# An attention and gating network on one core: weight conversion in four steps, and SyncE's queue in program order

## The chip, the cores and the metric

The kernel runs on one core of a Trainium2 chip. The metric is the device time of one execution in microseconds (us). TensorE (PE) does the matrix products, VectorE (DVE) and ScalarE (ACT) the work on single elements, GpSimd (POOL) a few small things, and SyncE (SP) issues most DMA transfers. Each engine works through its own instructions in order and waits for the others by semaphores.

## What is computed

Three stages follow each other, on 4 batches, 448 tokens, 12 heads of 64:

```python
scores = q @ k.T / sqrt(64) - log(448)
x = sigmoid(scores) @ v                       # heads joined: 4 x 448 x 768
h = relu(x @ w_in); u, v = h[:512], h[512:]   # on the last axis
x = (u * (w_spatial @ layernorm(v) + b)) @ w_out
theta = x @ w_theta
y = x + w_tok_r @ (x * cos(theta)) + w_tok_i @ (x * sin(theta))
out = y + relu(y @ w_ch)
```

The weights come as 64-bit floats, q, k, v as 32-bit floats.

## The kernel before

**Products.** A 32-bit operand is split into a hi part, rounded to the format that TensorE multiplies fast, and a lo part, the rest; a product is three matmuls (hi hi, hi lo, lo hi). The hi part of a weight is a copy on ScalarE, the lo part a subtraction on VectorE.

**The attention stage** has 12 rounds, `r` = 0 to 11 (L363 to L403), three for each batch; a round takes two tiles of two heads each. In a round TensorE does, for the round after it (`nxt`), the scores of the last 64 rows (`end_scores`, tile `pse`), then for its own two tiles the product with v (`begin_attend`, `attend`, tile `psa`), then the scores of `nxt` (`scores`, tile `pss`, three for each tile). ScalarE makes a sigmoid of each score tile (L187) and copies each result to `X` (L60); VectorE makes the lo part of `X` and a small copy `XL` (L233). There are three score tiles in PSUM, so that the fourth matmul group of a round waits for a sigmoid. `split_pair` (L178) makes hi and lo of the keys and queries `kqr` of the round after next (`aft`), on VectorE. When the three rounds of a batch are through, its u and v products (`uv`, tile `psd`, with the parts `wih` and `wil` of `w_in`) are put on the list `todo`, and `uv_now` runs as many as `UV_BY` names for the round, once enough pieces are `finished`.

**The weight conversion** runs beside this. 39 pieces (12 of `w_in`, 27 of later weights) are loaded as 64-bit numbers (`load`, L96, tile `wraw`, four buffers) and turned into 32-bit ones by bit operations: `low` (two instructions on VectorE, L105 and L107, tile `wq`), `high` (ScalarE, L112, in place in `wraw`, so behind `low`), `join` (VectorE, L117, behind `high`). A piece of `w_in` then gets its hi part (`part_high`, L286, ScalarE) and its lo part (`part_low`, L290, VectorE, behind the hi part); any other piece is written to memory as 32-bit numbers (L282, called a spill here). `begin_pieces` and `end_pieces` are a step: in one step the pieces loaded before get `low` and `high`, and the pieces that had these before get join, hi part and lo part. A round has two steps, from round 3 on three.

**Order.** Inside the block at L347 the instructions of TensorE, ScalarE and VectorE stand in the order of the code. SyncE's DMAs are ordered by a planner, and can go out ahead of what stands before them in the code. Behind the block the planner orders all engines.

Of the kernel before, what the change touches and what calls it, by code (L numbers as in the profile page):

```python
# [18 lines left out]
B, H, S, D = 4, 12, 448, 64  # L19
NP = H // 2  # L20
# [18 lines left out]
CH_FROM = (1, 0)  # L39
NX = 12  # L40
NKQ = 3
UV_BY = (0, 0, 0, 3, 5, 7, 10, 13, 15, 18, 20)
NW = 4
NQ = 4
# [4 lines left out]
def net(ctx: ExitStack, tc: tile.TileContext, kq, vd, vl, w_in, w_sp, bsp, w_out, w_th, w_tok, w_ch, ident, out):  # L49
# [3 lines left out]
    def sub(o, a, b):  # L53
        ve.tensor_tensor(out=o, in0=a, in1=b, op=ALU.subtract)  # L54
# [23 lines left out]
    for i in range(2):  # L78
        t = const.tile([P, DH], F32R, name=f"vb{i}")
# [62 lines left out]
    def chunks(w):  # L142
        return w.rearrange("(c p) f -> p c f", p=P)
# [22 lines left out]
    def load_kq(n):  # L166
        b, p = divmod(n, NP)
        t = {"n": n, "a": {}, "fs": n in F32_SCORES}
        r = t["r"] = at.tile([P, 2, S], F32, tag="kqr", name="kqr", bufs=4)
        nc.sync.dma_start(r, kq[b, p])  # L170
        return t
# [6 lines left out]
    def split_pair(t):  # L178
        r = t["r"]
        hi = t["h"] = at.tile([P, 2, S], F32R, tag="kqh", name="kqh", bufs=NKQ)  # L180
        lo = t["l"] = at.tile([P, 2, S], F32R, tag="kql", name="kql", bufs=NKQ)
        ve.tensor_copy(hi, r)
        sub(lo, r, hi)

    def sigmoid(tag, ps, bufs):
        af = at.tile([P, 2, S], F32, tag=tag, name="af", bufs=bufs)
        se.activation(af, ps[:, :, :S], AF.Sigmoid, bias=bias, scale=1.0 / math.sqrt(D))  # L187
        return af

    def scores(t, g):  # L190

        ps = ps_s.tile([P, 2, 512], F32, tag="s", name="pss")
        c = slice(g * P, (g + 1) * P)
        if t["fs"]:
            for j, a in enumerate(halves):
                te.matmul(ps[:, j, :S], t["r"][a, 0, c], t["r"][a, 1, :], start=True, stop=True)
        else:
            for n, (w, x) in enumerate(("hh", "hl", "lh")):
                for j, a in enumerate(halves):
                    te.matmul(ps[:, j, :S], t[w][a, 0, c], t[x][a, 1, :], start=n == 0, stop=n == 2)  # L200
        t["a"][g] = sigmoid("af", ps, NAF)

    def end_scores(ts):

        ps = ps_s.tile([P, 2, 512], F32, tag="s", name="pse")
        for i, t in enumerate(ts):
            for j, a in enumerate(halves):
                te.matmul(ps[halves[i], j, :S], t["r"][a, 0, L0:S], t["r"][a, 1, :], start=True, stop=True)
        return sigmoid("afe", ps, 2)
# [3 lines left out]
    def begin_attend(ts, ends, ae):  # L213

        ps = [ps_m.tile([P, 512], F32, tag="m", name="psa") for _ in ts]
        for i, t in enumerate(ts):
            for j, a in enumerate(halves):
                te.matmul(ps[i][a, :S], ends[halves[i], t["n"] % NP // 2 * 2 + j, :], ae[halves[i], j, :],
                          start=True, stop=False)
        return ps  # L220
# [15 lines left out]
    def uv(b, g):  # L236
        ps = ps_m.tile([P, 512], F32, tag="m", name="psd")
        if g < 4:
            for k in range(KC):
                if g < 3:  # L240
                    xh, xlo = (xs[b, k][:, i, g * P:(g + 1) * P] for i in range(2))
                else:
                    xh, xlo = (xl[b // 2, k][:, i].rearrange("p b t -> p (b t)") for i in range(2))
                te.matmul(ps, xh, wih[:, k, DH:], start=k == 0, stop=False)
                te.matmul(ps, xh, wil[:, k, DH:], start=False, stop=False)
                te.matmul(ps, xlo, wih[:, k, DH:], start=False, stop=k == KC - 1)
            r = x_p.tile([P, DH], F32, tag="ev", name="ev", bufs=2)
            acopy(r, ps, AF.Relu)
            if g < 3:
                nc.scalar.dma_start(v_d[b][g * P:(g + 1) * P, :], r)  # L250
            else:
                nc.scalar.dma_start(v_d[b - 1][L0:S, :], r[0:64])
                nc.scalar.dma_start(v_d[b][L0:S, :], r[64:P])
        else:
            f = g - 4
            fs = slice(f * P, (f + 1) * P)
            for k in range(KC):
                X = xs[b, k]
                mm3(ps[:, :S], wih[:, k, fs], wil[:, k, fs], X[:, 0, :], X[:, 1, :], k == 0, k == KC - 1)
            r = x_p.tile([P, DH], F32, tag="ev", name="ev", bufs=2)  # L260
            acopy(r[:, :S], ps[:, :S], AF.Relu)
            nc.scalar.dma_start(u_d[b][fs, :], r[:, :S])
# [29 lines left out]
    pieces = [Piece(chunks(w_in), k, slice(o, o + DH)) for o in (DH, 0) for k in range(KC)]  # L292
# [12 lines left out]

    loaded, apart, joined = [], [], []
    todo = []
    N = B * NP
    finished = 0

    def load_pieces(n):
        for _ in range(n):
            if pieces:
                loaded.append(pieces.pop(0))
                loaded[-1].load()

    def begin_pieces(n):
        joined[:] = apart
        apart[:] = loaded
        loaded.clear()  # L320
        for w in joined:
            w.join()
        for w in apart:
            w.low()
        load_pieces(n)

    def end_pieces():
        nonlocal finished
        for w in apart:
            w.high()  # L330
        for w in joined:
            w.part_high()
        for w in joined:
            w.part_low()
        finished += len(joined)
        joined.clear()

    def uv_now(n):
        nonlocal groups
        for _ in range(n):  # L340
            if todo and finished >= (KC if todo[0][1] < 4 else 2 * KC):
                uv(*todo.pop(0))
                groups += 1

    R = B * NP // 2
    groups = 0
    with tc.manual_schedule(engines={mybir.EngineType.PE, mybir.EngineType.Activation, mybir.EngineType.DVE}):  # L347
        rounds = {r: [load_kq(2 * r + i) for i in range(2)] for r in range(1)}
        load_pieces(1)
        ends = load_ends(0)  # L350
        rounds[1] = [load_kq(2 + i) for i in range(2)]
        for t in rounds[0]:
            load_v(t)
        split_pair(rounds[0][1])
        for g in range(3):
            scores(rounds[0][0], g)
        ae = end_scores(rounds[0])
        for t in rounds[1]:
            split_pair(t)
        for g in range(3):  # L360
            scores(rounds[0][1], g)
        nc.sync.dma_start(idt, ident)
        for r in range(R):  # L363
            b, q = divmod(r, NP // 2)
            cur, nxt, aft = rounds.pop(r), rounds.get(r + 1), None
            last = r == R - 1
            if nxt:
                ends_n = load_ends(b + 1) if q == NP // 2 - 1 else ends
                ae_n = end_scores(nxt)
            begin_pieces(1)  # L370
            ps = begin_attend(cur, ends, ae)
            for t, o in zip(cur, ps):
                attend(t, o)
            if nxt:
                for t in nxt:
                    load_v(t)
                ends, ae = ends_n, ae_n
            if r + 2 < R:
                aft = rounds[r + 2] = [load_kq(2 * (r + 2) + i) for i in range(2)]
            if nxt:  # L380
                for g in range(3):
                    scores(nxt[0], g)
                for g in range(3):
                    scores(nxt[1], g)
            end_pieces()
            if q == NP // 2 - 1:
                todo += [(b, g) for g in range(8) if g != 3 or b % 2]
            if last:
                break
            if r >= NP // 2:  # L390
                begin_pieces(2 if r == NP // 2 else 1)
                if aft:
                    split_pair(aft[0])
                uv_now(1)
                end_pieces()
            elif aft:
                split_pair(aft[0])
            begin_pieces(1 if r < NP // 2 - 1 else 2)
            if aft:
                split_pair(aft[1])  # L400
            uv_now(UV_BY[r] - groups - 1)
            end_pieces()
            uv_now(UV_BY[r] - groups)  # L403
        while pieces or loaded or apart:
            begin_pieces(2)
            end_pieces()
    es_l.close()
# [259 lines left out]
    for b in range(B):  # L667
# [4 lines left out]
        for k in range(KC):  # L672
            nc.scalar.dma_start(yf[:, k, :], src[:, k, :])
            t = pc.tile([P, 2, S], F32R, tag="Y", name="Y", bufs=6)
# [3 lines left out]
        for e in range(KC):  # L678
# [4 lines left out]
            r = po.tile([P, S], F32, tag="o", name="o")  # L683
# [49 lines left out]
```

## Time and profile before

| | us |
|---|---|
| median of 3 runs | 656.89 |
| lowest and highest of them | 656.76, 657.71 |
| the profiled execution | 658.28 |
| its span, first to last instruction | 656.5 |

The profile comes from one execution. Its times are us from the start of the span; idle time stands in square brackets with what ended it. PEclk is the granted clock of TensorE as a share of full speed. Round r begins where the matmuls of L208 for round r+1 begin.

### The profile page before, as it was taken

What the parts mean: (1) busy time and instruction counts of PE and PEld (TensorE: products, weight loads), DVE (VectorE), ACT (ScalarE), POOL (GpSimd) and SP (SyncE); (2) the same over time, 40 slices, a digit from 0 to 9 for tenths busy, and PEclk for the clock granted to TensorE, in tenths of its full rate; (3) what the DMA queues carried; (4) which work ended last, traced back from release to release, by engine and by line L of the source; (5) the groups of instructions that cost most, each with busy time, mean ns of one, the idle gap of its engine ahead of it and who ended that gap; (6) DMA issues with size and microseconds to landing.
All of it is one profiled execution on the core that took longest, in us unless ns stands there. A gap on an engine that the chain in (4) does not pass through costs nothing.

```text
span 656.5 us, 9127 instructions
## 1 busy us (share of the span) xinstructions
PE 641.8 (98%) x3434; PEld 524.3 (80%) x3434; DVE 384.1 (59%) x747; ACT 286.0 (44%) x468; POOL 8.0 (1%) x18
## 2 busy tenths in 40 slices
PE   7999979999999999999999999999999999999997
PEld 3545656567656688899999999999999999899996
DVE  3657763545355368783315699998678765523311
ACT  5776546535553544274312554664344333302200
POOL 2000000000000000100000000000000000000000
PEclk9989979999999999999999999999999999999999
DMA  8754744685545466566454223351121012623411
GB/s 319 240 195 148 262 133 150 223 263 173 160 167 203 161 212 192 173 184 191 154 171 160 91 62 101 90 183 42 43 85 42 1 43 75 207 86 125 141 65 62
DMA packets 52368, 94.78 MB, mean 144 GB/s; under 512 B 8290, under 2 KB 38884, under 8 KB 52324
## 3 DMA queue, kind: packets, MB, share of 16 engines
q1 hardware_dynamic: 41060, 75.84, 35.8%
q10 hardware_dynamic: 11264, 18.36, 8.5%
q8 instruction: 27, 0.44, 0.3%
q14 instruction: 17, 0.14, 0.1%
HBM read 64.79 MB, written 29.39 MB: 143 GB/s over the span
## 4 chain that ended last, share of the span: by engine, by line
PE 87%; DVE 4%; ACT 3%; DMA 3%; issue 2%; POOL 0%; ACTq 0%; DVEq 0%; POOLq 0%
PE psa L225 7%; PE pss L200 5%; PE py L617 5%; PE py L618 5%; PE py L616 5%; PE pch L64 5%; PE pch L65 5%; PE pt L575 4%; PE pt L576 4%; PE pt L577 4%; PE pch L63 4%; PE ppo L65 3%; PE ppo L63 3%; PE ppo L64 3%; PE psd L63 2%; PE psd L65 2%
## 5 line engine op out<-in xcount | busy, mean ns | idle before, releaser
L187 ACT ACTIVATE af<-pss,bias 128x896 f32<-128x896 f32 x72 | 66.1, 1018 | 2.4 <-PE pss L200 2.4
L575 PE MATMUL pt<-thh,XT 128*128 128x384 f32 x168 | 58.2, 346 | 0.0
L225 PE MATMUL psa<-af,vr 128*64 128x448 f32 x288 | 56.8, 543 | 0.0
L577 PE MATMUL pt<-thh,XT 128*128 128x384 f32 x168 | 56.3, 335 | 0.0
L576 PE MATMUL pt<-thl,XT 128*128 128x384 f32 x168 | 56.3, 335 | 0.0
L64 PE MATMUL pch<-Y,wch 128*128 128x448 f32 x144 | 52.8, 369 | 0.4 <-DVE Y L54 0.4
L65 PE MATMUL pch<-Y,wcl 128*128 128x448 f32 x144 | 52.7, 368 | 0.0
L63 PE MATMUL pch<-Y,wch 128*128 128x448 f32 x144 | 52.2, 368 | 0.0
L117 DVE SCALAR_TENSOR_TENSOR wq<-wraw,wq 128x384 int32<-128x384 int32 (+2 forms) x51 | 29.6, 594 | 35.0 <-ACT wraw L112 34.6
L225 PEld LDWEIGHTS psa<-af,vr 128*64 128x64 f32 x288 | 19.6, 137 | 36.3 <-issue 34.5
L684 DVE SCALAR_TENSOR_TENSOR o<-pch,yf 128x448 f32<-128x448 f32 x24 | 15.0, 624 | 54.6 <-PE pch L65 54.6
L586 ACT ACTIVATE m<-r 128x384 f32<-128x384 f32 x28 | 14.6, 522 | 62.7 <-DVE r L584 62.3
L63 PE MATMUL psd<-X,wih 128*128 128x448 f32 x96 | 37.0, 385 | 3.3 <-ACT wih L60 3.2
L112 ACT ACTIVATE wraw<-wraw 128x384 f32<-128x384 f32 (+2 forms) x51 | 29.6, 604 | 22.3 <-DVE wq L105 16.8
L54 DVE TENSOR_TENSOR X<-psa,X 128x448 fp32r<-128x448 f32 x24 | 14.9, 623 | 38.6 <-ACT X L60 38.6
L65 PE MATMUL psd<-X,wil 128*128 128x448 f32 x96 | 36.2, 377 | 0.7 <-DVE wil L54 0.6
L60 ACT ACTIVATE ev<-psd 128x448 f32<-128x448 f32 (+1 forms) x30 | 17.0, 568 | 45.3 <-PE psd L65 19.9
L64 PE MATMUL psd<-X,wih 128*128 128x448 f32 x96 | 35.9, 374 | 0.0
L60 ACT ACTIVATE Y<-yf 128x448 fp32r<-128x448 f32 x24 | 13.9, 579 | 49.3 <-DMA yf<-y_d 28.9
L63 PE MATMUL ppo<-g,wbh 128*128 128x448 f32 x96 | 35.2, 366 | 0.0
L64 PE MATMUL ppo<-g,wbh 128*128 128x448 f32 x96 | 35.1, 366 | 0.0
L65 PE MATMUL ppo<-g,wbl 128*128 128x448 f32 x96 | 35.1, 366 | 0.0
(138 smaller groups left out, 1514.7 us busy)
## 6 DMA issues: line engine op xcount, KB each, us to landing
kqr<-in_kq SPq DMA_DIRECT2D x24, 448.0 KB, 5.0
wraw<-in_w_in SPq DMA_DIRECT2D x12, 512.0 KB, 5.4
x_d<-x ACTq DMA_DIRECT2D x24, 224.0 KB, 2.4
xf<-x_d SPq DMA_DIRECT2D x4, 1344.0 KB, 6.3
y_d<-y SPq DMA_DIRECT2D x24, 224.0 KB, 1.9
yf<-y_d ACTq DMA_DIRECT2D x24, 224.0 KB, 3.5
out_t<-o SPq DMA_DIRECT2D x24, 224.0 KB, 2.0
vr<-in_vd SPq DMA_DIRECT2D x24, 192.0 KB, 4.1
```

The source lines that it names most:

```text
L63: te.matmul(ps, wh, xh, start=first, stop=False)
L64: te.matmul(ps, wh, xl, start=False, stop=False)
L65: te.matmul(ps, wl, xh, start=False, stop=last)
L187: se.activation(af, ps[:, :, :S], AF.Sigmoid, bias=bias, scale=1.0 / math.sqrt(D))
L200: te.matmul(ps[:, j, :S], t[w][a, 0, c], t[x][a, 1, :], start=n == 0, stop=n == 2)
L225: te.matmul(ps[a, :S], t["v"][:, 2 * c + j, :], t["a"][c][:, j, :], start=False, stop=c == 2)
L575: te.matmul(o, t[:, k, 0, :], thh[:, k, hs], start=k == 0, stop=False)
L576: te.matmul(o, t[:, k, 0, :], thl[:, k, hs], start=False, stop=False)
L577: te.matmul(o, t[:, k, 1, :], thh[:, k, hs], start=False, stop=k == KC - 1)
L616: te.matmul(o, z[:, 0, ds], tkh[:, c, :], start=i == 0 and n == 0, stop=False)
L617: te.matmul(o, z[:, 0, ds], tkl[:, c, :], start=False, stop=False)
L618: te.matmul(o, z[:, 1, ds], tkh[:, c, :], start=False, stop=i == 3)
```

## The change

- The steps of a piece become four: load; `low` and `high`; join and hi part; lo part. `begin_pieces` first makes the lo parts of the pieces whose hi part was made in the step before, and counts them as finished; `end_pieces` makes hi parts, then `high`.
- In each round `end_pieces` of the first step stands directly behind `begin_pieces`, ahead of the attend matmuls and the X copies (before: behind the scores).
- Two pieces are loaded ahead of round 0 instead of one, both ahead of the v ends and of the second pair of keys and queries. `LOADS` gives the pieces of the second and third step of a round.
- Keys and queries of round r+3 are loaded in round r (before, in the code: of round r+2); v of round r+2 is loaded in round r (before: of r+1). The buffers stay four each.
- SyncE's DMAs inside the block stand in the order of the code, too.

```diff
@@ -39,6 +39,7 @@
 CH_FROM = (1, 0)
 NX = 12
 NKQ = 3
+LOADS = ((1, 0), (2, 0), (2, 0), (2, 2)) + 7 * ((1, 2),)
 UV_BY = (0, 0, 0, 3, 5, 7, 10, 13, 15, 18, 20)
 NW = 4
 NQ = 4
@@ -305,7 +306,6 @@
 
     loaded, apart, joined = [], [], []
     todo = []
-    N = B * NP
     finished = 0
 
     def load_pieces(n):
@@ -315,6 +315,11 @@
                 loaded[-1].load()
 
     def begin_pieces(n):
+
+        nonlocal finished
+        for w in joined:
+            w.part_low()
+        finished += len(joined)
         joined[:] = apart
         apart[:] = loaded
         loaded.clear()
@@ -325,15 +330,11 @@
         load_pieces(n)
 
     def end_pieces():
-        nonlocal finished
+
+        for w in joined:
+            w.part_high()
         for w in apart:
             w.high()
-        for w in joined:
-            w.part_high()
-        for w in joined:
-            w.part_low()
-        finished += len(joined)
-        joined.clear()
 
     def uv_now(n):
         nonlocal groups
@@ -344,17 +345,18 @@
 
     R = B * NP // 2
     groups = 0
-    with tc.manual_schedule(engines={mybir.EngineType.PE, mybir.EngineType.Activation, mybir.EngineType.DVE}):
-        rounds = {r: [load_kq(2 * r + i) for i in range(2)] for r in range(1)}
-        load_pieces(1)
+    with tc.manual_schedule(engines={mybir.EngineType.PE, mybir.EngineType.Activation, mybir.EngineType.DVE, mybir.EngineType.SP}):
+        rounds = {0: [load_kq(i) for i in range(2)]}
+        load_pieces(2)
         ends = load_ends(0)
         rounds[1] = [load_kq(2 + i) for i in range(2)]
-        for t in rounds[0]:
+        for t in rounds[0] + rounds[1]:
             load_v(t)
         split_pair(rounds[0][1])
         for g in range(3):
             scores(rounds[0][0], g)
         ae = end_scores(rounds[0])
+        rounds[2] = [load_kq(4 + i) for i in range(2)]
         for t in rounds[1]:
             split_pair(t)
         for g in range(3):
@@ -362,46 +364,42 @@
         nc.sync.dma_start(idt, ident)
         for r in range(R):
             b, q = divmod(r, NP // 2)
-            cur, nxt, aft = rounds.pop(r), rounds.get(r + 1), None
-            last = r == R - 1
+            cur, nxt, aft = (rounds.get(r + i) for i in range(3))
             if nxt:
                 ends_n = load_ends(b + 1) if q == NP // 2 - 1 else ends
                 ae_n = end_scores(nxt)
+            if r + 3 < R:
+                rounds[r + 3] = [load_kq(2 * (r + 3) + i) for i in range(2)]
             begin_pieces(1)
+            end_pieces()
             ps = begin_attend(cur, ends, ae)
             for t, o in zip(cur, ps):
                 attend(t, o)
-            if nxt:
-                for t in nxt:
+            if aft:
+                for t in aft:
                     load_v(t)
-                ends, ae = ends_n, ae_n
-            if r + 2 < R:
-                aft = rounds[r + 2] = [load_kq(2 * (r + 2) + i) for i in range(2)]
-            if nxt:
-                for g in range(3):
-                    scores(nxt[0], g)
-                for g in range(3):
-                    scores(nxt[1], g)
-            end_pieces()
             if q == NP // 2 - 1:
                 todo += [(b, g) for g in range(8) if g != 3 or b % 2]
-            if last:
+            if not nxt:
                 break
-            if r >= NP // 2:
-                begin_pieces(2 if r == NP // 2 else 1)
-                if aft:
-                    split_pair(aft[0])
-                uv_now(1)
-                end_pieces()
-            elif aft:
+            ends, ae = ends_n, ae_n
+            for t in nxt:
+                for g in range(3):
+                    scores(t, g)
+            begin_pieces(LOADS[r][0])
+            if aft:
                 split_pair(aft[0])
-            begin_pieces(1 if r < NP // 2 - 1 else 2)
+            end_pieces()
+            uv_now(min(1, UV_BY[r] - groups))
+            if LOADS[r][1]:
+                begin_pieces(LOADS[r][1])
             if aft:
                 split_pair(aft[1])
-            uv_now(UV_BY[r] - groups - 1)
-            end_pieces()
+            uv_now(min(1, UV_BY[r] - groups))
+            if LOADS[r][1]:
+                end_pieces()
             uv_now(UV_BY[r] - groups)
-        while pieces or loaded or apart:
+        while pieces or loaded or apart or joined:
             begin_pieces(2)
             end_pieces()
     es_l.close()
```

## Rows read from the trace of the kernel before

**Rows 1.** The page: busy us (share of the span) and instructions of each engine.

```profile
PE 641.8 (98%) x3434; PEld 524.3 (80%) x3434; DVE 384.1 (59%) x747; ACT 286.0 (44%) x468; POOL 8.0 (1%) x18
```

**Rows 2.** TensorE's waits (us, times, longest), up to 98.28 us; last row: from there on.

```profile
PE psd L63 <- ACT wih L60: 3.2, 2, 2.0
PE pss L200 <- ACT af L187: 1.9, 3, 0.9
...
PE pch L64 <- DVE Y L54: 0.4, 1, 0.4
```

**Rows 3.** Windows r1 to r5 (r3 in two): us; PE, PEld, DVE, ACT, POOL; PEclk; DMA.

```profile
22.97:34.03 11.06, 10.97 (x77) 5.21 (x77) 7.11 (x13) 9.15 (x13) 0.00 (x0) 1.00 0.59 188
34.03:47.38 13.35, 11.94 (x76) 5.73 (x76) 9.34 (x16) 9.99 (x14) 0.00 (x0) 0.92 0.63 210
47.38:59.54 12.16, 11.58 (x78) 5.40 (x76) 9.66 (x17) 8.80 (x14) 0.00 (x0) 0.95 0.54 187
59.54:72.60 13.06, 12.84 (x56) 9.98 (x54) 10.11 (x18) 8.27 (x14) 0.00 (x0) 1.00 0.52 169
72.60:98.28 25.68, 21.72 (x113) 13.41 (x112) 16.49 (x31) 12.39 (x18) 0.00 (x0) 0.87 0.57 175
98.28:116.68 18.40, 18.35 (x113) 11.99 (x112) 6.80 (x14) 10.68 (x15) 0.00 (x0) 1.00 0.53 162
```

**Rows 4.** TensorE's timeline: start us, us; r0, r2 and r4.

```profile
11.91 0.98 PE L208 MATMUL pse<-kqr 64*64 64x448 f32 x8
...
35.69 4.73 PE L225 MATMUL psa<-af,vr 128*64 128x448 f32 x24
...
90.65 0.74 PE L63 MATMUL psd<-X,wih 128*128 128x448 f32 x1 [1.96 <-ACT wih L60]
```

**Rows 5.** ScalarE's timeline in r2.

```profile
40.20 0.69 ACT L112 ACTIVATE wraw<-wraw 128x512 f32<-128x512 f32 x1 [3.36 <-DVE wq L105]
...
42.20 0.96 ACT L60 ACTIVATE X<-psa 128x448 fp32r<-128x448 f32 x2
```

**Rows 6.** VectorE's timeline in r2.

```profile
36.88 0.69 DVE L54 TENSOR_TENSOR wil<-wq,wih 128x512 fp32r<-128x512 f32 x1 [4.29 <-ACT wih L60]
37.48 0.62 DVE L182 CAST kqh<-kqr 128x896 fp32r<-128x896 f32 x1
...
39.15 0.68 DVE L117 SCALAR_TENSOR_TENSOR wq<-wraw,wq 128x512 int32<-128x512 int32 x1
39.75 0.42 DVE L105 TENSOR_SCALAR wq<-wraw 128x512 int32<-128x512 uint32 x1
...
40.81 0.62 DVE L182 CAST kqh<-kqr 128x896 fp32r<-128x896 f32 x1
```

**Rows 7.** SyncE's waits from 17 to 98 us.

```profile
SPq L170 <- DVE kql L54: 17.5, 6, 7.9
```

**Rows 8.** The page's DMA issues: KB each, median us to landing.

```profile
kqr<-in_kq SPq DMA_DIRECT2D x24, 448.0 KB, 5.0
wraw<-in_w_in SPq DMA_DIRECT2D x12, 512.0 KB, 5.4
```

**Rows 9.** SyncE's timeline at the start; the first row is kq2 and kq3.

```profile
2.60 1.31 SPq L170 DMA_DIRECT2D kqr<-in_kq  x2
...
6.73 0.43 SPq L96 DMA_DIRECT2D wraw<-in_w_in  x1
```

**Rows 10.** Tile kqr, from issue to landing: kq2 (issued 2.60), then kq3 (3.15).

```profile
DMA to landing us min/median/max: 8.0/8.0/8.0
...
DMA to landing us min/median/max: 8.6/8.6/8.6
```

**Rows 11.** Windows: scores of r1, scores of r2, the stretch behind them; columns as rows 3.

```profile
29.36:34.03 4.67, 4.58 (x38) 3.00 (x37) 3.12 (x7) 4.31 (x6) 0.00 (x0) 1.00 0.77 221
40.42:45.00 4.58, 3.17 (x25) 1.95 (x24) 4.51 (x8) 4.58 (x8) 0.00 (x0) 1.00 0.91 292
45.00:48.50 3.50, 3.49 (x20) 2.12 (x24) 1.35 (x4) 3.50 (x5) 0.00 (x0) 0.53 0.72 281
```

## The prediction

> **What bounds the kernel now.** First the page: TensorE is busy 641.8 of 656.5 us [rows 1], so all that a new order can win is TensorE's idle time and what it runs at half clock. Then TensorE's waits, cut at 98.28 us, where round 5 begins: behind that point it waits 0.4 us in all; ahead of it the rows show 3.2 us for hi parts of `w_in` from ScalarE and 1.9 us for sigmoids [rows 2]. So only the first rounds (r0 to r4) can change. Then the same stretch cut by rounds [rows 3]; round r begins with the end-row matmuls of round r+1. r1 takes 11.06 us. r2 takes 13.35, r3 12.16 up to its first u/v group and 13.06 from there, r4 25.68. r5 runs what r4 runs (the same attention, two u groups) in 18.40, so r4 loses 25.68 - 18.40 = 7.28 us. The TensorE timeline shows where: inside the first u group, which waits for `wih` [rows 4]; the granted clock of that round is 0.87 [rows 3].
>
> Why the parts are late is seen on ScalarE and VectorE in r2. The three-step order makes them hand one piece to and fro: the lo part (VectorE, L290) waits 4.29 us for the hi part, which stands behind six sigmoids; then come a split, a join and a `low`; only after that `low` can ScalarE run `high`, having stood idle 3.36 us [rows 5, 6]. Behind that `high` stand the end rows' sigmoid, the X copies and the next sigmoids, and through them TensorE's score buffers. In r4 the same chain holds the parts that the u group needs.
>
> **The change, part by part.** No instruction is added or taken away: 39 pieces, each with a load, two instructions in `low`, a `high`, a join and either two parts or a spill, in both versions. Each round keeps its u/v groups: followed through both loops, the condition on `finished` gives the running counts 0, 0, 0, 3, 5, 7, 10, 13, 15, 18, 20 either way. What changes is order.
>
> *Four steps.* The lo part goes one step later, ahead of the next join, and `end_pieces` of a round's first step goes ahead of the X copies. So each operation uses what the other engine made a step earlier. In r4 the hi part of piece 11 (the last of u) is then first on ScalarE behind the end rows' sigmoid, and its lo part first on VectorE behind the X copies. The first u group starts some 10.9 us into that round, more than 3 us after both. The wait goes, and with it the half clock. Worth: 7.28 us, with r5 as the measure. What is late next in r4 is nothing I can find, as in r5.
>
> *The early rounds* become bound by VectorE. Start-to-start times there [rows 6]: lo part 0.60, split 1.67, join 0.60, `low` 1.06. Before r3's first X copy ScalarE now has two `high`, each behind its `low`. From r2's X to that point VectorE does 3 lo parts, 3 joins, 3 `low` and 2 splits: 1.8 + 1.8 + 3.2 + 3.3 = 10.1 us. The walk: r0 begins at 13.05 (the start, below); r0 and r1 go at r1's pace, to 35.1; r2's attend ends 6.3 us later (34.03 to 40.4 before [rows 3, 4]), X is through on both engines at 44.0 and r3 begins at 46.3. VectorE is done at 44.0 + 10.1 = 54.1, the last `high` 0.6 later, two X copies take 0.9: r3's sigmoids begin at 55.6. TensorE's attend ends at 46.3 + 6.3 = 52.6, so they could have begun at 53.5: TensorE stands 2.1 us before its fourth score tile, and the first u/v group starts at 59.0. From r2's start that is 23.9 us against 13.35 + 12.16 = 25.51: 1.6 gained. The 0.22 us of waits from there to r4 (13.06 less 12.84 of busy TensorE [rows 3]) goes too, as piece 5 is done a round earlier. Bounds of this part: 0, if r3 falls back by another 1.8, and 3.7, if VectorE's slip doesn't reach TensorE.
>
> *Keys and queries ahead.* Worth nothing. `kqr` still has four buffers, and before, SyncE already issued each load as its buffer came free: from 17 to 98 us these waited 17.5 us for the split that frees the buffer [rows 7], and no split waited for a load. The cover is the round between load and split; without it a split would wait a load's whole way, 5.0 us [rows 8].
>
> *SyncE's order.* Its DMAs now stand in program order: in each round kq, a weight load, v, then spills and loads. Spills wait for a join, v for the attend matmuls; behind them stands the next weight load, wanted a step later. The tightest place I find is r4 to r10, where the `low` at a round's start gate the X copies. Their loads go out about 14.5 us into an 18.4 us round, behind the second step's join; a 512 KB load takes 5.4 us [rows 8], the 384 KB here some 0.3 less, so they land 1.2 us into the next round. Wanted is 2.7 us into it (u copy, `high`, join ahead): 1.5 us of margin, cost 0. The identity and the earlier v loads have rounds of cover.
>
> *The start.* Before, the second weight load went out at 6.73, behind all four key loads [rows 9]. Now it stands ahead of kq2 and kq3. These landed at 2.60 + 8.0 = 10.6 and 3.15 + 8.6 = 11.75 [rows 9, 10], 1.15 us for 448 KB, so 512 KB more ahead of them is 1.3 us. kq3 then lands at 13.05; TensorE asked for it at 11.91 [rows 4]. Cost 1.14 us. Bounds: 0, if transfers don't land in turn, and 2.8, if that idle time also drops the clock (next).
> The Trainium skill (DMA: Bandwidth & Descriptors, Queues, rings and completion order) says that completion is not first-in-first-out per issuing engine; taken far, kq3 need not wait, the term is 0 and the sum 1.14 us lower. The two landings above came in turn.
>
> *The clock.* In r1 TensorE waits for sigmoids in short steps and is granted 1.00; in r2, with longer gaps, it is busy 3.17 of 4.58 us, and the next 3.5 us are granted 0.53 [rows 11], half clock (1.2 of 2.4 GHz) for nearly all of it. The 2.1 us gap of r3 is longer than r2's, so I take one such fall: 3.5 us at half clock cost about 1.7. Bounds 0, and 3.4 for a second fall.
> The Trainium skill (TensorE: Matmul & The Clock Gate, A second HAM failure mode: psum-queue depth-cycling) says that micro-idling between groups of matmuls, as they cycle through PSUM, is enough to make the clock oscillate. By it every score stretch paced by ScalarE would fall, r0 and r1 too, 3.4 us more; r1's row does not agree, r2's does.
>
> **Sum** against the profiled execution: -7.28 - 1.6 - 0.22 + 1.14 + 1.7 = -6.3 us. Its span of 656.5 becomes 650.2, its time of 658.28 becomes 652.0. That execution stands 1.4 us above the median of 656.89, so the median becomes **650.6**.
>
> **Rivals.** (a) Start and clock cost nothing: -9.1, 647.8. For it: r1's full clock at a stuttering TensorE. Against it: the 10.1 us of VectorE. (b) The wait only moves: VectorE falls so far behind in r3 and r4 that the u group still waits. It decides if the lo part of piece 11 is over 3 us late, and gives back most of the 7.28: about 656. Against it: r5 needs 6.80 us of VectorE in 18.40 [rows 3]. (c) Slower: SyncE's fixed order makes weight loads late. A load behind a spill goes out only after a join that waits for a `high` behind six sigmoids; if it lands 3 us later than I take, 1.5 beyond the margin, then `low`, `high`, X copies and sigmoids are late by that in each of r4 to r10, and TensorE with them: 7 x 1.5 = 10.5 us, 661.1. From 2.4 us late (0.9 a round) it takes back all that the change wins. Against it: the margin, and that a load wanted this early has the DMA queue nearly to itself. (d) The change doesn't do what it says: the key loads gain no lead; that is in the forecast and changes no time. Behind the last round nothing is fixed by hand, and a planner that starts from other times may set things a little differently; this only widens the range.
>
> **How the numbers follow.** The forecast has 0.62, with a range of its own of 648.5 to 653; (a) 0.18; (b) 0.11, half of it within 0.2%; (c) 0.09. A measurement tells about 0.2%, 1.3 us, from no change. Faster takes the forecast, (a) and some of (b): 0.84; same 0.07; slower 0.09. The range runs from 0.6 us below (a), 647.2, to 654.6: with the start's and the clock's upper bounds the sum is -7.28 - 1.6 - 0.22 + 2.8 + 3.4 = -2.9, 654.0, and 0.6 goes to the planner.
>
> **What would show it.** Right: r4 near 18.4 us; no u/v matmul waits for `wih` or `wil`; r2 near 11.2; r0's end-row matmuls wait for a key load about 1.1 us; TensorE stands near 2 us before the fourth score tile of r3, with `high` on ScalarE waiting for a `low` ahead of the X copies. Wrong: in r4 to r10 a `low` that waits for its load, or TensorE waits behind r5 that weren't there.

## The result, and the profile after

The changed kernel takes 647.36 us (median of 4 runs, 646.19 the lowest) against 656.94 before, a ratio of 0.9846 with an interval of 0.9827 to 0.9865: about 10.1 us less, where 6.3 were forecast. The direction is right; by the ratio the time is 646.8, 0.4 us below the range's lower end. One of the 4 executions, the profiled one, had a granted clock of 0.755 from end to end and took 779.85; it is left out of the ratio, and the profile below is that of a further run of the same kernel (647.45, ratio 0.9848, 0.9835 to 0.9861; span 645.5). Lines below L42 have moved by one in it: L209 is the end rows' matmul, L61 the hi copy, L55 the lo part, L113 `high`.

The page's engine line, which answers to [rows 1]:

```profile
PE 636.0 (99%) x3434; PEld 522.6 (81%) x3434; DVE 384.6 (60%) x747; ACT 286.3 (44%) x468; POOL 8.0 (1%) x18
```

TensorE's waits in the whole span (us, times, longest), the answer to [rows 2]:

```profile
PE pss L197 <- DMA kqr<-in_kq: 3.9, 1, 3.9
PE psd L64 <- ACT ev L61: 0.6, 2, 0.3
PE pss L201 <- ACT af L188: 0.5, 1, 0.5
PE pch L65 <- DVE Y L55: 0.4, 1, 0.4
```

The same instructions and 5.8 us less of busy TensorE: 5.3 less in r1 to r4 (69.05 to 63.76 us), where the clock was 0.93 on average and is 1.00 now, and 1.8 less in the last stage, whose pace differs from one execution to another (see the end); the rest of the span takes 1.3 more. No wait of TensorE for `wih` or `wil` is left. The windows by rounds, r0 to r4 (r3 in two) and r5, columns as in [rows 3]:

```profile
11.97:23.60 11.63, 11.55 (x77) 5.51 (x77) 9.59 (x18) 8.78 (x12) 0.00 (x0) 1.00 0.87 315
23.60:34.66 11.06, 10.98 (x77) 5.21 (x77) 10.03 (x18) 10.21 (x15) 0.00 (x0) 1.00 0.75 228
34.66:45.71 11.05, 10.98 (x76) 5.21 (x76) 10.33 (x19) 10.32 (x15) 0.00 (x0) 1.00 0.85 283
45.71:57.21 11.50, 10.96 (x76) 5.21 (x77) 10.77 (x20) 10.57 (x16) 0.00 (x0) 1.00 0.71 238
57.21:69.68 12.47, 12.47 (x57) 10.06 (x55) 9.87 (x17) 6.25 (x11) 0.00 (x0) 1.00 0.44 137
69.68:88.10 18.42, 18.37 (x114) 11.94 (x113) 9.97 (x19) 10.58 (x15) 0.00 (x0) 1.00 0.66 216
88.10:106.49 18.39, 18.35 (x113) 11.98 (x112) 10.34 (x20) 10.76 (x15) 0.00 (x0) 1.00 0.75 238
```

Round 5 begins at 88.10 instead of 98.28, 10.18 us earlier: r4 gives 25.68 - 18.42 = 7.26, r2 13.35 - 11.05 = 2.30, r3 0.66 up to its first u/v group and 0.59 behind it, and the start takes back 0.63 (r1 begins at 23.60 instead of 22.97). The clock is 1.00 throughout. From r5 to the last stage TensorE takes 465.6 us against 464.6 (553.66 - 88.10 and 562.93 - 98.28, the last stage's first matmul less r5's start); in the other runs below this stretch lies between 464.2 and 466.4, so the difference can't be put down to the change.

One sign that the forecast named for being wrong did appear. With SyncE's queue in program order a `low` waits for its load three times in r4 to r10, by 0.53, 0.59 and 1.28 us; here is the longest, on VectorE:

```profile
153.30 0.36 DVE L106 TENSOR_SCALAR wq<-wraw 128x384 int32<-128x384 uint32 x1 [1.28 <-DMA wraw<-in_w_th]
```

So the margin of 1.5 us that the forecast gave these loads was not there. TensorE had no wait behind any of them, and with SyncE planned again (below) none of them occurs, at the same time.

What the forecast feared for r3 stands in VectorE's and ScalarE's timelines, much smaller. VectorE from r2's X to r3's, then ScalarE ahead of r3's X copies (answers to [rows 6] and [rows 5]):

```profile
41.75 0.62 DVE L55 TENSOR_TENSOR X<-psa,X 128x448 fp32r<-128x448 f32 x1
42.40 0.23 DVE L234 CAST XL<-X 128x128 fp32r<-128x128 f32 x1
42.54 0.69 DVE L55 TENSOR_TENSOR wil<-wq,wih 128x512 fp32r<-128x512 f32 x1
...
52.06 0.69 DVE L108 SCALAR_TENSOR_TENSOR wq<-wraw,wq 128x512 int32<-128x512 int32 x1
```

```profile
52.11 0.68 ACT L113 ACTIVATE wraw<-wraw 128x512 f32<-128x512 f32 x1 [0.24 <-ACT wraw L113]
52.70 0.95 ACT L61 ACTIVATE X<-psa 128x448 fp32r<-128x448 f32 x2
53.54 5.50 ACT L188 ACTIVATE af<-pss,bias 128x896 f32<-128x896 f32 x6
```

VectorE works from 42.54 to 52.7 with no idle time on its way, 10.1 us, as walked. But r2's X is through at 42.5, not at 44.0, and the last `high` (52.11) runs beside the second instruction of the last `low` (52.06), not behind it. So the X copies start at 52.70 and the sigmoids of r3 at 53.54, where attend ends at 45.71 + 6.3 = 52.0, and TensorE's wait is 0.48 us:

```profile
54.60 0.47 PE L201 MATMUL pss<-kqh 64*128 64x448 f32 x2 [0.48 <-ACT af L188]
```

### The profile page after: what moved, and what is told of

Its sections match the earlier page's. It is cut to its first block, busy times and chain, and to the rows that moved or that the text cites. A ratio compares the mean times of both kernels' runs of the same rounds, so it can differ in the third digit from the quotient of the medians.

```text
span 778.1 us, 9127 instructions
## 1 busy us (share of the span) xinstructions
PE 770.4 (99%) x3434; PEld 561.1 (72%) x3434; DVE 387.1 (50%) x747; ACT 289.1 (37%) x468; POOL 7.9 (1%) x18
## 4 chain that ended last, share of the span: by engine, by line
PE 99%; DMA 0%; DVE 0%; issue 0%; DVEq 0%
PE psa L226 9%; PE pss L201 7%; PE py L615 5%; PE py L616 5%; PE py L614 5%; PE pch L66 5%; PE pch L65 5%; PE pt L573 5%; PE pt L575 5%; PE pt L574 5%; PE pch L64 4%; PE psd L245 3%; PE psd L64 3%; PE psd L66 3%; PE ppo L66 3%; PE ppo L64 3%
## 5 line engine op out<-in xcount | busy, mean ns | idle before, releaser
L226 PE MATMUL psa<-af,vr 128*64 128x448 f32 x288 | 73.7, 675 | 0.0
L573 PE MATMUL pt<-thh,XT 128*128 128x384 f32 x168 | 67.2, 400 | 0.0
L574 PE MATMUL pt<-thl,XT 128*128 128x384 f32 x168 | 64.9, 387 | 0.0
L575 PE MATMUL pt<-thh,XT 128*128 128x384 f32 x168 | 64.9, 386 | 0.0
L65 PE MATMUL pch<-Y,wch 128*128 128x448 f32 x144 | 60.1, 420 | 0.2 <-DVE Y L55 0.2
L66 PE MATMUL pch<-Y,wcl 128*128 128x448 f32 x144 | 60.3, 421 | 0.0
L64 PE MATMUL pch<-Y,wch 128*128 128x448 f32 x144 | 59.7, 421 | 0.0
L61 ACT ACTIVATE ev<-psd 128x448 f32<-128x448 f32 (+1 forms) x30 | 17.1, 569 | 92.4 <-PE psd L66 50.3
L55 DVE TENSOR_TENSOR X<-psa,X 128x448 fp32r<-128x448 f32 x24 | 15.0, 624 | 70.6 <-ACT X L61 70.4
L118 DVE SCALAR_TENSOR_TENSOR wq<-wraw,wq 128x384 int32<-128x384 int32 (+2 forms) x51 | 29.5, 596 | 40.8 <-ACT wraw L113 40.5
L578 DVE TENSOR_SCALAR m<-pt 128x384 f32<-128x384 f32 x28 | 15.6, 557 | 56.1 <-PE pt L575 56.1
L64 PE MATMUL psd<-X,wih 128*128 128x448 f32 x96 | 40.8, 425 | 0.0
L64 PE MATMUL ppo<-g,wbh 128*128 128x448 f32 x96 | 40.6, 423 | 0.0
L65 PE MATMUL ppo<-g,wbh 128*128 128x448 f32 x96 | 40.4, 421 | 0.0
L66 PE MATMUL psd<-X,wil 128*128 128x448 f32 x96 | 40.4, 421 | 0.0
L66 PE MATMUL ppo<-g,wbl 128*128 128x448 f32 x96 | 40.3, 420 | 0.0
L65 PE MATMUL psd<-X,wih 128*128 128x448 f32 x96 | 40.0, 417 | 0.0
L61 ACT ACTIVATE Y<-yf 128x448 fp32r<-128x448 f32 x24 | 13.8, 578 | 61.6 <-DMA yf<-y_d 53.5
```

The lines of the kernel that those rows point to most:

```text
L64: te.matmul(ps, wh, xh, start=first, stop=False)
L65: te.matmul(ps, wh, xl, start=False, stop=False)
L66: te.matmul(ps, wl, xh, start=False, stop=last)
L226: te.matmul(ps[a, :S], t["v"][:, 2 * c + j, :], t["a"][c][:, j, :], start=False, stop=c == 2)
L573: te.matmul(o, t[:, k, 0, :], thh[:, k, hs], start=k == 0, stop=False)
L574: te.matmul(o, t[:, k, 0, :], thl[:, k, hs], start=False, stop=False)
```

## The experiments

The change was taken apart into the **early end** (E: the first step's `end_pieces` ahead of the X copies), the **fourth step** (S), the **loads ahead** (L: two pieces ahead of round 0, two in round 1's second step), and the rest (K): SyncE's fixed order, the earlier key and v loads, and the places of the splits and of the first u/v group among the steps (in the changed code's r0 to r2 a step's beginning stands ahead of the first split, and its end ahead of the second). Each run's ratio is to the kernel before on the same chip; on the chips used it took 656.9 to 657.7 us (medians), so the medians can be compared too. The round lengths are differences of the starts of the end rows' matmuls in each run's TensorE timeline.

| parts | ratio (interval) | median us | r1 begins | r2 | r3 | r4 |
|---|---|---|---|---|---|---|
| none | 1 | 656.94 | 22.97 | 13.35 | 25.22 | 25.68 |
| E | 0.9822 (0.9798 to 0.9846) | 645.76 | 23.00 | 11.06 | 23.72 | 18.54 |
| S | 0.9924 (0.9910 to 0.9937) | 652.33 | 22.98 | 11.06 | 23.44 | 24.19 |
| L | 0.9956 (0.9943 to 0.9969) | 654.70 | 24.90 | 12.84 | 28.82 | 18.96 |
| E S | 0.9822 (0.9802 to 0.9843) | 645.85 | 23.13 | 11.06 | 23.45 | 18.42 |
| E L | 0.9880 (0.9864 to 0.9895) | 649.47 | 24.19 | 11.39 | 24.76 | 18.41 |
| E S L | 0.9847 (0.9834 to 0.9860) | 647.50 | 24.76 | 11.06 | 23.97 | 18.40 |
| E S K | 0.9824 (0.9811 to 0.9838) | 645.87 | 23.02 | 11.07 | 23.44 | 18.41 |
| S L K | 0.9888 (0.9873 to 0.9903) | 649.93 | 24.47 | 11.51 | 27.18 | 18.40 |
| E L K | 0.9928 (0.9915 to 0.9941) | 652.77 | 23.64 | 13.01 | 25.98 | 18.42 |
| E S L K, the change | 0.9848 (0.9835 to 0.9861) | 647.45 | 23.60 | 11.05 | 23.97 | 18.42 |

**The changed kernel at full clock.**

> The changed kernel as it is, for a profile at full clock. Measured before this run: about 10 us faster than the kernel before, where the forecast was 6.3 (7.28 from round 4, 1.6 and 0.2 from rounds 2 and 3, less 1.14 at the start and 1.7 for one fall of the clock). Theory 1 (the gains are as sized, the two costs did not come): the granted clock stays at 1.00 in all of rounds 0 to 4, the end-row matmuls of round 0 start near 11.9, round 5 begins near 89.2 (98.28 - 9.1). Theory 2 (the start cost came, VectorE's slip in rounds 2 and 3 did not): round 0 starts near 13.0, rounds 1, 2 and 3 each take about 11.06 up to the u/v groups, no TensorE gap before round 3's fourth score tile.

Measured above. Theory 1 holds for the clock and for r0's start; r5 began at 88.10, earlier still than its 89.2. Theory 2 holds for r2 at 11.05, not for r3, where a gap of 0.48 us is left. Both costs that the forecast charged shrank in this execution: 0.63 us at the start, 0.48 in r3.

**The second load later.**

```diff
-        load_pieces(2)
+        load_pieces(1)
...
+        load_pieces(1)
```

(the second line behind the v loads)

> The second weight load goes back behind kq3 and the v loads; all else as changed. If the load ahead of kq2 and kq3 costs TensorE 1.14 us at the start, this is 1.1 us faster than the changed kernel and round 0 begins near 11.9; if transfers don't land in turn, or TensorE isn't held by kq3, no difference (within 0.3 us).

0.9825 (0.9812 to 0.9839), 645.82: 1.6 us faster than the changed kernel. r0 takes 23.40 - 12.34 = 11.06, without the 0.57 more that it takes in the changed kernel; r0 itself began later (12.34), since the matmuls ahead of it took longer in this execution (the end rows at 8.76 took 1.52 us, against 0.98 in the kernel before, at a granted clock of 1.00 in both; why is not known). So the load ahead of kq2 and kq3 costs r0 something; what the rest of the 1.6 is, this run alone doesn't say. In two more profiles of the changed code (SyncE planned, and the one beside E and E S) r5 begins at 89.12 and 88.90, so that the 88.10 above is an early one and the 87.90 here 0.2 to 1.2 us ahead.

**SyncE planned again.**

```diff
-... mybir.EngineType.DVE, mybir.EngineType.SP}):
+... mybir.EngineType.DVE}):
```

> SyncE is taken out of the hand-ordered engines; all else as changed. If SyncE's fixed order is worth nothing, or costs only the start: the same time within 1.2 us, or up to 1.1 us faster. If the order by hand is a part of the gain (rival: planned DMAs come late for the pipeline of four steps), 2 us or more slower, with VectorE's low waiting for a weight load.

0.9842 (0.9829 to 0.9856), 647.46: the same. SyncE's fixed order is worth nothing here.

**Three steps in the changed kernel** (E L K).

```diff
 def begin_pieces(n):
-    for w in joined:
-        w.part_low()
...
 def end_pieces():
+    for w in apart:
+        w.high()
     for w in joined:
         w.part_high()
-    for w in apart:
-        w.high()
+    for w in joined:
+        w.part_low()
```

> The lo part goes back into the step of its hi part (three steps again); the early first end_pieces, the loads ahead and SyncE's order stay. If the fourth step takes away the wait of round 4, it comes back in part: VectorE waits for hi parts behind the sigmoids again, 3 to 8 us slower than the changed kernel. If the early end_pieces or the earlier loads did it, no more than 1 us slower.

652.77, 5.3 us slower than the changed kernel, but not where the forecast put it: r4 is 18.42, and r1 to r3 are slow (12.49, 13.01, 25.98). VectorE in r3, where the lo part waits for a hi part behind the sigmoids, and a split waits behind it; then ScalarE, idle until the next `low` is through (the first row names no releaser, but VectorE's L106 of that piece had ended 0.08 us earlier, at 55.89), with the X copies behind it:

```profile
51.99 1.29 DVE L55 TENSOR_TENSOR wil<-wq,wih 128x512 fp32r<-128x512 f32 x2 [1.10 <-ACT wih L61]
53.20 0.62 DVE L183 CAST kqh<-kqr 128x896 fp32r<-128x896 f32 x1
```

```profile
55.97 0.69 ACT L113 ACTIVATE wraw<-wraw 128x512 f32<-128x512 f32 x1 [2.60 <-issue]
57.04 0.70 ACT L113 ACTIVATE wraw<-wraw 128x512 f32<-128x512 f32 x1 [0.37 <-DVE wq L106]
```

So r4's 7.26 us don't hang on the fourth step. That raised theory F (the loads ahead clear r4) against G (the forecast's).

**Loads ahead alone** (L), with two edits to the kernel before.

```diff
-        load_pieces(1)
+        load_pieces(2)
...
-            begin_pieces(1 if r < NP // 2 - 1 else 2)
+            begin_pieces(1 if r < 1 else 2)
```

> The kernel before with one edit: two pieces loaded ahead of round 0 and two in round 1's second step, so that each piece is made as early as in the changed kernel, in three steps. Theory F (the two pieces ahead take away round 4's wait, the fourth step the hand-to-fro of rounds 1 to 3): round 4 takes about 18.4 us instead of 25.68, rounds 1 to 3 stay slow or get slower, 3 to 7 us faster than the kernel before. Theory G (as predicted: the fourth step takes away round 4's wait): round 4 keeps most of its 7.28 us, the time stays within 2 us of the kernel before.

654.70. r4 is 18.96, as F said, but r3 grows from 25.22 to 28.82: two pieces more ahead of the u group clear it, and the same work in r3 costs half of that again. TensorE waits 2.22 us for a sigmoid there, and the windows of r3 show a clock of 0.84:

```profile
48.87:64.34 15.47, 12.56 (x76) 6.52 (x76) 12.17 (x22) 11.39 (x16) 0.00 (x0) 0.84 0.55 174
```

**The change without its loads ahead** (E S K): `load_pieces(1)`, and `LOADS` begins `((1, 0), (1, 0), (2, 0), (2, 2))`.

> The changed kernel with one edit: one piece ahead of round 0 and one in round 1's second step, as in the kernel before; four steps, early end, SyncE's order stay. Theory F: the parts of the last u piece come after round 4's sigmoids, so that its u group waits; 1 to 4 us slower than the changed kernel, all of it in round 4. Theory G: round 4 stays near 18.4 us, the time within 1 us of the changed kernel or faster by the start's 0.6.

645.87, 1.6 us faster than the changed kernel; r2, r3 and r4 take 11.07, 23.44 and 18.41, together as short as in any run. F falls: with early end and fourth step the loads ahead aren't needed, and they cost. G is not proved by it, since E is in this run.

**The fourth step alone** (S): the change's edits of `begin_pieces` and `end_pieces`, and `or joined` in the last loop, put into the kernel before.

> The kernel before with one edit: four steps (the lo part one step later, hi parts ahead of high). end_pieces stays behind the scores, loads and SyncE's planned order as before. Theory F: rounds 2 and 3 lose their waits (about 3 us faster), round 4 still waits for the last u piece and keeps a part of its 7.28: 650 to 655. Theory G: all waits go, 647 to 650.

652.33. r1 to r3 are clean (11.07, 11.06, 23.44), r4 still takes 24.19: 5.8 us over its pace. TensorE's timeline in r4, then ScalarE's:

```profile
84.46 0.48 PE L63 MATMUL psd<-X,wih 128*128 128x448 f32 x1 [0.79 <-ACT wih L60]
87.39 0.74 PE L65 MATMUL psd<-X,wil 128*128 128x448 f32 x1 [2.26 <-DVE wil L54]
```

```profile
81.15 1.18 ACT L60 ACTIVATE wih<-wq 128x512 fp32r<-128x512 f32 x2
82.19 1.15 ACT L112 ACTIVATE wraw<-wraw 128x512 f32<-128x512 f32 x2
83.77 0.63 ACT L60 ACTIVATE wih<-wq 128x512 fp32r<-128x512 f32 x1 [0.43 <-DVE wq L117]
```

Both steps' hi parts still stand behind r4's six sigmoids (81.15). So the fourth step by itself doesn't clear r4, and theory G falls with it.

**The change without its early end** (S L K).

```diff
-            end_pieces()
             ps = begin_attend(cur, ends, ae)
...
+            end_pieces()
             begin_pieces(LOADS[r][0])
```

> The changed kernel with one edit: the first step's end_pieces goes back behind the scores. If the early end matters (high must be done a step ahead, else VectorE's next join waits for it behind the sigmoids): VectorE waits at L118 in rounds 0 to 3, 1 to 4 us slower than the changed kernel. If the fourth step alone suffices: within 0.7 us; by the forecast's walk even faster by up to 2 us, since no high stands ahead of the X copies.

649.93, 2.5 us slower than the changed kernel, as expected, but not where: VectorE waits at L118 once (5.49 us in r1, which costs TensorE nothing), and it is r3 that takes 27.18. There TensorE waits at the first u/v group for VectorE's X, which stands behind work for the pieces, and the clock falls behind that (windows around 60.16):

```profile
60.16 0.50 PE L245 MATMUL psd<-wih,X 128*128 128x512 f32 x1 [1.63 <-DVE X L55]
```

```profile
54.80:60.16 5.36, 3.69 (x31) 2.15 (x27) 5.26 (x10) 5.36 (x7) 0.00 (x0) 1.00 0.82 246
60.16:67.00 6.84, 6.84 (x23) 5.52 (x24) 6.74 (x13) 4.19 (x8) 0.00 (x0) 0.75 0.79 269
```

**The kernel before, again.**

> The kernel before, unchanged, for a second profile. In its first profile the matmuls of the last stage started 206.6 ns apart, in every other profile so far 202.7, which makes that stage 1.7 us longer. If that belongs to the kernel, it comes again (last stage 90.2 us); if it belongs to the one execution, the last stage takes 88.4 us and the span is near 654.8. Rounds 2 to 4 as before: 13.35, 25.2, 25.7 us.

1.0006 (0.9991 to 1.0022); the last stage's matmuls start 203 ns apart here, so its slower pace belongs to an execution. The span was 656.6 all the same: r3 took 25.75 and r4 26.58 us this time. r2 took 12.79, with nearly the same gaps before its score tiles (0.50 and 0.90 us, before 0.51 and 0.87), but no fall of the clock behind them. These are the stretches that the forecast's term for the clock rests on, the second and third of [rows 11], in this execution:

```profile
40.92:45.50 4.58, 3.18 (x25) 1.95 (x24) 4.51 (x8) 4.58 (x8) 0.00 (x0) 1.00 0.88 293
45.50:49.00 3.50, 3.42 (x30) 1.50 (x30) 1.36 (x4) 3.50 (x5) 0.00 (x0) 1.00 0.72 283
```

**The early end alone** (E).

```diff
             begin_pieces(1)
+            end_pieces()
             ps = begin_attend(cur, ends, ae)
...
                     scores(nxt[1], g)
-            end_pieces()
```

> The kernel before with one edit: the first step's end_pieces directly behind its begin_pieces; three steps. Theory H (the fourth step clears rounds 2 and 3, the early end clears round 4): round 4 takes about 18.4 us, rounds 1 to 3 lose as much as before or more, since the X copies now stand behind the hand-to-fro (some 5 us over r1's pace): 650 to 654. Rival: without the fourth step the u group's parts stay late and round 4 keeps its 7 us: 656 or more.

645.76, faster than either theory gave: r4 is clear as H said, and r2 and r3 as well (11.06, 23.72), where H expected losses. Moving one call does all that the change does, and 1.3 us more (647.02 for the changed kernel on the same chip). ScalarE in r2, then TensorE's attend matmuls:

```profile
36.75 1.04 ACT L187 ACTIVATE af<-pse,bias 128x896 f32<-128x896 f32 x1
38.59 0.69 ACT L112 ACTIVATE wraw<-wraw 128x512 f32<-128x512 f32 x1 [0.80 <-DVE wq L105]
39.18 0.61 ACT L60 ACTIVATE wih<-wq 128x512 fp32r<-128x512 f32 x1
39.70 0.52 ACT L60 ACTIVATE X<-psa 128x448 fp32r<-128x448 f32 x1
40.51 0.55 ACT L60 ACTIVATE X<-psa 128x448 fp32r<-128x448 f32 x1 [0.28 <-PE psa L225]
41.37 5.50 ACT L187 ACTIVATE af<-pss,bias 128x896 f32<-128x896 f32 x6 [0.31 <-PE pss L200]
```

```profile
35.73 4.73 PE L225 MATMUL psa<-af,vr 128*64 128x448 f32 x24
```

The hand-to-fro is still there (0.80 us for a `low`), but it stands while TensorE is in its attend matmuls and needs nothing of ScalarE. The second X copy waits for TensorE, not TensorE for it. In r4 the last u piece's parts still come behind the sigmoids, but just in time, and the round takes 18.54. ScalarE, VectorE and the matmuls that use the two parts:

```profile
81.88 0.67 ACT L60 ACTIVATE wih<-wq 128x512 fp32r<-128x512 f32 x1
```

```profile
82.58 0.69 DVE L54 TENSOR_TENSOR wil<-wq,wih 128x512 fp32r<-128x512 f32 x1 [2.24 <-ACT wih L60]
```

```profile
82.89 0.36 PE L63 MATMUL psd<-X,wih 128*128 128x448 f32 x1
...
83.33 0.47 PE L65 MATMUL psd<-X,wil 128*128 128x448 f32 x1
```

The hi part is done 0.3 us before TensorE takes it, the lo part with nothing to spare (82.58 + 0.69 = 83.27). In the kernel before, ScalarE's part of this piece's step began only when VectorE had been through the step ahead of it. VectorE, then ScalarE, in r4 before:

```profile
86.86 1.29 DVE L54 TENSOR_TENSOR wil<-wq,wih 128x512 fp32r<-128x512 f32 x2 [6.35 <-ACT wih L60]
```

```profile
89.53 0.56 ACT L112 ACTIVATE wraw<-wraw 128x384 f32<-128x384 f32 x1 [2.18 <-DVE wq L105]
```

**Early end and fourth step** (E S), the two sets of edits together.

> The kernel before with these two edits, and no others: planned SyncE, key loads, piece loads all as before. If the two make the whole gain: rounds 0 to 4 at 11.06, 11.06, 11.06, 23.44, 18.4 us, 645.5 to 647, no slower than the changed kernel. If the key loads ahead or SyncE's fixed order are part of it: over 1 us slower than the changed kernel, with VectorE or TensorE waiting for a DMA in rounds 1 to 5.

645.85: no faster than E alone; r3 is 0.27 us shorter, r0 0.27 longer. With K on top (E S K) it is 645.87, so with four steps K is worth nothing.

**The changed kernel beside these.**

> The changed kernel once more, on the same chip as the run before it, for a direct comparison: 647.4 as in the earlier runs, rounds 0 and 3 about 0.5 us over the others' pace each.

647.02 (646.66 to 650.35).

**Early end and loads ahead** (E L), and **with the fourth step** (E S L): the edits of L on top of the runs above.

> The kernel before with the early end and the two pieces ahead; three steps, planned SyncE, key loads as before. Theory L (the pieces ahead put more VectorE and ScalarE work into rounds 0 to 3, which are full, and only the fourth step makes room for it): rounds 1 to 3 slow as in the run with three steps (12.5, 13.0, 26.0 us), about 652. Rival (SyncE's fixed order or the earlier key loads made that run slow): 645.5 to 647.

> The kernel before with the early end, four steps and the two pieces ahead: the changed kernel without its earlier key and v loads and without SyncE's fixed order. Theory L: as the changed kernel, near 647.2, with round 3 about 0.5 us over and a longer round 0. Rival: 645.8, as with one piece ahead.

649.47 and 647.50. Theory L holds in kind: the pieces ahead cost 3.7 us with three steps and 1.6 with four, and E S L is as long as the whole change (647.45). Its size for three steps, 652, does not: in E L, r3 is 1.0 us longer than in E, TensorE waiting 1.27 us for a sigmoid, but r1 to r3 are less slow than in the run with E L K (652.77). So with three steps K costs 3.3 us. Its DMAs don't show as the cause: from 14 to 100 us of that run VectorE, ScalarE and TensorE wait for no DMA. What differs is that a step's end stands ahead of the second split: there the lo parts of r3 wait 1.10 us for a hi part with the split behind them (51.99, 53.20), in E L the split stands ahead of them and they don't wait, and TensorE's waits for a sigmoid in r1, r2 and r3 are 1.38, 1.87 and 2.50 us against 0, 0.24 and 1.27. No run moved the split by itself.

## Why the prediction was right or wrong

The direction was right and so was the largest term, r4. Two steps of the sum failed, the walk of the early rounds and the fall of the clock; and the cause named for r4 was the wrong one of two.

**Where the time was: right.** All of it came from r2 to r4, 7.26 us of it from r4 (7.28 forecast), and behind r5 only the two stretches differ that differ between executions of one kernel. With four steps the key loads and SyncE's order are worth nothing, as forecast: without SyncE's order 647.46 against 647.45, without all of K 647.50 against 647.45 and 645.85 against 645.87. With three steps K costs 3.3 us (652.77 against 649.47). Rival (c) did not come, though its margin of 1.5 us was not there. Rival (a), which gave 647.8, is nearest to what the profile shows, with a start that costs something and early rounds that cost less.

**"Four steps ... The wait goes": wrong in its cause.** The forecast took the lo part's later step and the moved `end_pieces` as one edit and put r4's 7.28 us on the pipeline of four. What it said of r4 came true in the changed kernel: the last u piece's hi part starts at 71.69, its lo part at 77.50, and the first u group, at 80.59, 10.9 us into the round, waits for neither. But that took the pieces ahead as well: in E S K, without them, the two start at 81.20 and 81.89, behind the sigmoids, and r4 is clear all the same. Alone, the fourth step leaves 5.8 us of the wait; alone, the early end takes all of it, and the loads ahead nearly all (18.96). In the kernel before, the ScalarE work of two steps stood back to back behind six sigmoids, so the second step's `high` could only start when VectorE had gone through the work of the first: in r4 two lo parts, two joins and a `low` (86.86 to 89.5), in r2 a lo part, a split, a join and a `low`. The early end puts one of the two steps into the attend matmuls. The fourth step takes the same chain out of r2 and r3 in another way; with E it adds nothing unless L puts more work there.

**"The early rounds": mis-sized,** 1.6 forecast up to the first u/v group, 2.96 measured. VectorE's 10.1 us were right, but two other parts of the walk were not. It let r2's X end 8.9 us after r2 began; it was 7.9 (34.66 to 42.5), for the second X copy waited for TensorE (41.10), not for a `high`. And it charged 0.6 us for a `high` behind VectorE's last `low`, which ran beside it. So r3's sigmoids began 18.9 us after r2 did instead of 20.5, and TensorE stood 0.48 us instead of 2.1. The walk's 59.0 is also some 0.3 us early: it stands 3.4 us behind the sigmoids' start, where 3.67 were measured (53.54 to 57.21), so that the walk should have given 1.3. Behind the first u/v group 0.59 came instead of 0.22: the wait for `wil` there held two matmuls 0.69 us apart (63.08, 63.77) whose neighbours stand 0.23 apart, which is 0.46, where the row of idle time counts 0.22.

**"The clock": the term of 1.7 us did not come.** TensorE stood 0.48 us, not 2.1, and was granted 1.00 throughout. But the runs don't bear out that a stop of about 2 us brings one fall. It did in S L K (1.63 us ahead of the first u/v group, then 0.75) and in L (2.22 us; r3 at 0.84). In E L K it did not: stops of 1.38, 1.87 and 2.50 us, and a clock of 1.00 in all of r1 to r4. The longest of them and the window from there:

```profile
60.05 0.47 PE L201 MATMUL pss<-kqh 64*128 64x448 f32 x2 [2.50 <-ACT af L188]
```

```profile
60.05:75.12 15.07, 15.02 (x72) 11.51 (x72) 10.99 (x20) 8.84 (x13) 0.00 (x0) 1.00 0.48 152
```

And the fall in r2 of the kernel before, on which the term was modelled, is missing in that kernel's second profile. So the term belongs to an execution as much as to a stop; what decides it was not found. The Trainium skill (TensorE: Matmul & The Clock Gate, A second HAM failure mode: psum-queue depth-cycling) says of another kernel that TensorE idled for moments between its groups often enough for the clock to oscillate; in the changed kernel r1 and r2 idle 0.08 and 0.07 us between their groups at a clock of 1.00, so these rows show no such fall.

**"The start": 1.14 forecast, 0.63 measured** in r0 of this profile, but one profile doesn't settle it. In the other runs with both pieces loaded first, r1 began 0.7 to 1.9 us later than in the kernel before (1.45 in the second profile of the changed kernel); in the others at most 0.2 later, except two whose first matmuls took longer: 0.4 with the second load later, and 0.5 in the second profile of the kernel before itself. VectorE's second split, which waits for kq2, shows the DMA's share: it started at 11.35 to 12.69 in the runs with both pieces first, at 9.38 to 10.94 in the others. So the cost is real, inside the bounds, and differs from one execution to another.

The sum, by the terms: 1.7 (clock) + 1.36 (early rounds) + 0.37 + 0.51 (start) - 0.02 = 3.92 us more than the 6.26 forecast, the 10.18 by which r5 begins earlier. Both ends of that come from one profile each; in the second profile of the kernel before r5 begins at 99.65, 1.4 us later.

**The best version** is the kernel before with `end_pieces` moved (645.76, 0.9822); fourth step, loads ahead, earlier key loads and SyncE's order can stay out. Its r4 has no time to spare for the last u piece; with the fourth step added (645.85) the time is the same.

## What to carry to other kernels

When two engines hand work to and fro, look where in the round the exchange stands before making its pipeline deeper: moved into a stretch in which the bounding engine needs neither, a three-step chain cost 0.3 us in r3 and nothing elsewhere that shows in the median. Work taken ahead is not free where its engines are full: two pieces ahead cleared r4's wait where nothing else did, and cost 1.6 to 3.7 us where the early end had cleared it already. A change of several edits is to be costed edit by edit, also when one sentence seems to explain them all. And a loss that one profile shows, such as a fall of the clock, is worth a second profile before it becomes a term of a sum.

## What was not expected of the hardware

The same matmuls of the last stage ran at two paces at a granted clock of 1.00. The last stage of the profile before, then that of the changed kernel (windows, columns as in [rows 3]):

```profile
562.90:653.10 90.20, 89.71 (x433) 80.80 (x432) 29.09 (x50) 11.58 (x20) 0.00 (x0) 1.00 0.35 115
```

```profile
553.70:642.10 88.40, 87.93 (x433) 80.78 (x431) 28.96 (x49) 11.53 (x20) 0.00 (x0) 1.00 0.36 118
```

433 matmuls in 90.2 or 88.4 us. In the changed kernel's run beside E and E S the profiled execution (650.35) had the slow pace, the kernel before had the fast one in its second profile: it goes with the execution, not with the kernel. So of the 11.0 us between the two spans shown (656.5 and 645.5) 1.8 are none of the change's doing, and 1.0 is lost in the stretch before it, which differs between executions too. What sets the pace was not found.
